# Pooled attention and two feed-forward layers on one core: float64 words of the first block combined in a PSUM bank

## The chip, the cores and the metric

The kernel runs on one core of a Trainium2 chip. Its time is the device time of one execution, in microseconds (us); the median of several runs is given. TensorE multiplies matrices and writes to PSUM, a memory of eight banks of 128 x 512 float32 values. VectorE (DVE in the profile), ScalarE (ACT) and GpSimd (POOL) work on tiles in SBUF; VectorE and ScalarE also read and write PSUM. Each engine takes its instructions in order. The queue of the DMAs of this kernel is nearly always that of SyncE (SP).

## The reference, cut to what matters

q, k and v are 8 x 8 x 576 x 64 (batch, heads, sequence, head size).

```python
k_p = k.reshape(B, H, 72, 8, D).mean(axis=3)
v_p = v.reshape(B, H, 72, 8, D).mean(axis=3)
scores = matmul(q, k_p.T) / sqrt(D)
attn = exp(scores - max(scores)); attn = attn / (sum(attn) + 1e-9)
x = matmul(attn, v_p)                      # 4608 tokens x 512
g = s * relu(x @ w_in) ** 2 + b            # 2048 wide
x = g @ w_out                              # 512 wide
out = (sigmoid(x @ w_gate) * (x @ w_val)) @ w_out2      # 1536 wide, then 512
```

The activations come in float32, the five weights as float64. The result is float32.

## The kernel before, in words

**Products.** Every float32 product is made of three: each operand is split into a high part, rounded to the format that TensorE multiplies at full rate, and a low part, which is what rounding left over; high x low, high x high and low x high are added up in PSUM. The helper `split` (lines 53 to 56) makes the two parts: ScalarE copies the value into `hi` (line 55), and VectorE or GpSimd, as the caller says, subtracts (line 56).

**Weights.** A float64 weight tile arrives as 128 x 1024 words of 32 bits (`load64`, three buffers `raw`). `convert` (lines 73 to 84) makes a float32 of each pair of words, `low` and `high`, which lie alternately in SBUF: ScalarE turns the high word's exponent and leading mantissa bits into the middle value `w` (line 80), VectorE shifts the low word in place (line 81), combines `w` and `low` (line 82), and combines `high`'s sign bit and `w` (line 83). `w` is a tile `cv` of SBUF (six buffers). Lines 82 and 83 read two tensors each, both in SBUF. The weights `w_in` and `w_out` of the first feed-forward layer, 16 tiles each, are converted while block 0 runs, and split with GpSimd's subtraction: `split_wi` (lines 129 to 135) and `split_wo` (148 to 153). The split `w_in` is stored to DRAM for the other blocks, `w_out` stays in SBUF. The second layer's weights are converted and stored in the same way later on (`prep_w2`, from step 18 on).

**Order of the work.** The 4608 tokens are nine blocks of 512. The first layer runs in 144 steps (block j, slice m of the 2048). A step is `emit_h` (lines 186 to 206: 12 products into `hps`, then on ScalarE the Relu that reads `hps`, line 200, and the rest of the activation), `split_g`, and, two steps later, `emit_x` (lines 218 to 237: 12 products into the four accumulators `acc`). Attention makes the tokens of the following block in units of 256 tokens, two per block, a few pieces in each step, as the table `events` says (lines 445 to 482): `scores` twice per 128 tokens (a product into `sps`, a maximum and a subtraction on VectorE that read it, lines 370 and 371), `norm` (the sum and its inverse on VectorE, the product on GpSimd), `left`, `turn` twice (transposes into `tm` and `tl`, read by a split and a copy), and `values` twice (a product into `pv`, read by a split into `xh` and `xl`). `pool_v_pe` adds up the pooled rows of v for batches 0 and 1 with TensorE, into `vps`; `place_v` and `place_left` read it. Units 0 and 1, for block 0 itself, and the first conversions come ahead, in a stage in which all engines keep the order of the program (line 492). Units 2 and 3 belong to the 16 steps of block 0, and step 16 needs both. After that stage and up to step 16 every engine's order is planned at build time from a model of the durations; from step 16 on TensorE's order is that of the program (line 604).

**PSUM.** The eight banks are three pools: `ps_a` has four (the accumulators, and the scores of the first stage), `ps_b` two (`hps`, and batch 0's `vps`), and `ps_c` two (`sps`, `tm`, `tl`, `pv`, batch 1's `vps`). In the second layer (`first_half`, `plain`) the last two pools give two banks each to the products there. Whoever takes a bank waits until the last reader of what it held is done.

Of the kernel before, what the change touches and what calls it, by code (L numbers as in the profile page):

```python
# [8 lines left out]
F32 = mybir.dt.float32  # L9
F32R = mybir.dt.float32r  # L10
I32 = mybir.dt.int32
# [8 lines left out]
def pooled_attention_two_ffn(ctx, tc, q, k, v, v_left, w_in, w_out, s_in, b_in, w_gate, w_val, w_out2, out):  # L20
# [22 lines left out]
    cvp = ctx.enter_context(tc.tile_pool(name="cvp", bufs=6))  # L43
    dram = ctx.enter_context(tc.tile_pool(name="dram", bufs=1, space=DRAM))
    ps_a = ctx.enter_context(tc.tile_pool(name="ps_a", bufs=4, space=PSUM))
    ps_b = ctx.enter_context(tc.tile_pool(name="ps_b", bufs=2, space=PSUM))
    ps_c = ctx.enter_context(tc.tile_pool(name="ps_c", bufs=2, space=PSUM))

    ident = const.tile([128, 128], F32, name="ident")
    s_sb = const.tile([128, 1], F32, name="s_sb")  # L50
    b_sb = const.tile([128, 1], F32, name="b_sb")

    def split(hi, lo, src, eng):

# [18 lines left out]
    def convert(raw, w):  # L73

        words = raw.rearrange("p (f two) -> p f two", two=2)
        low, high = words[:, :, 0], words[:, :, 1]
        nc.scalar.activation(out=w.bitcast(F32), in_=high.bitcast(F32), func=ACTF.Copy, scale=2.0**-112)  # L80
        nc.vector.tensor_scalar(out=low, in0=low, scalar1=29, scalar2=None, op0=ALU.logical_shift_right)
        nc.vector.scalar_tensor_tensor(out=w, in0=w, scalar=3, in1=low, op0=ALU.logical_shift_left, op1=ALU.bitwise_or)
        nc.vector.scalar_tensor_tensor(out=w, in0=high, scalar=-(2**31), in1=w, op0=ALU.bitwise_and, op1=ALU.bitwise_or)
        return w.bitcast(F32)

    def block_of(t):
# [52 lines left out]
    def store_later():  # L139
        while later:  # L140
            dst, t = later.pop(0)
            nc.sync.dma_start(out=dst, in_=t if t.dtype == F32 else t.bitcast(F32))
# [43 lines left out]
    def emit_h(i):  # L186
        j, m = steps[i]
        n = blocks[j][1]
        hi, lo = wi.pop(i)
        ps = ps_b.tile([128, 512], F32, tag="b", name="hps")[:, :n]  # L190
        a, c = x_tiles(j)
        step = UNIT if i < 2 else n
        for t0 in range(0, n, step):
            f = slice(t0, t0 + step)
            for kk in range(KD):
                nc.tensor.matmul(out=ps[:, f], lhsT=hi[:, kk], rhs=c[:, kk, f], start=kk == 0, stop=False)  # L196
                nc.tensor.matmul(out=ps[:, f], lhsT=hi[:, kk], rhs=a[:, kk, f], start=False, stop=False)  # L197
                nc.tensor.matmul(out=ps[:, f], lhsT=lo[:, kk], rhs=a[:, kk, f], start=False, stop=kk == KD - 1)  # L198
        g = gp.tile([128, 512], F32, tag="g", name="g", bufs=2)[:, :n]
        nc.scalar.activation(out=g, in_=ps, func=ACTF.Relu)  # L200
        if j == 0:
            nc.scalar.activation(out=g, in_=g, func=ACTF.Square)
        else:
            nc.vector.tensor_tensor(out=g, in0=g, in1=g, op=ALU.mult)  # L204
        nc.scalar.activation(out=g, in_=g, func=ACTF.Identity, scale=s_sb, bias=b_sb)  # L205
        g_t[i] = g
# [95 lines left out]
    def pool_v_pe(b, what):  # L302

        n = NP if what == "v" else 2
        ps = (ps_c if b else ps_b).tile([128, n, D], F32, tag="c" if b else "b", name="vps")
        f = ps.rearrange("p i d -> p (i d)")
        ts = [raws.pop((b, nm)) for nm in (("v0", "v1") if what == "v" else ("l",))]
        per = POOL // len(ts)
        for r in range(POOL):
            t = ts[r // per]  # L310
            nc.tensor.matmul(out=f, lhsT=ident, rhs=t[:, r % per * n * D:(r % per + 1) * n * D], start=r == 0, stop=r == POOL - 1)
        sums[b, what] = ps
# [43 lines left out]
    def scores(u, t, c, pool=None):  # L356
        if c == 0:
            s_t[u, t] = (at2.tile([128, H, SP], F32, tag="e", name="e"), at2.tile([128, H], F32, tag="mx", name="mx"))
        e, mx = s_t[u, t]
        ps = (ps_a if pool else ps_c).tile([128, 4, SP], F32, tag="a" if pool else "c", name="sps")  # L360
        for i in range(2):
            for off, n, b, _ in segs(u * UNIT + t * 128, 128):
                nc.tensor.matmul(
                    out=ps[off:off + n, 2 * i:2 * i + 2, :].rearrange("p h j -> p (h j)"),
                    lhsT=q_t[u][:, 2 * i + c, t * 128 + off:t * 128 + off + n],
                    rhs=kbd[b % 2][:, 2 * i + c].rearrange("p two j -> p (two j)"),
                    start=True, stop=True,
                )
        h = slice(4 * c, 4 * c + 4)
        nc.vector.tensor_reduce(out=mx[:, h], in_=ps, axis=AX.X, op=ALU.max)  # L370
        nc.vector.tensor_tensor(out=e[:, h], in0=ps, in1=mx[:, h].unsqueeze(2).to_broadcast([128, 4, SP]),
                                op=ALU.subtract)
        if c == 1:
            nc.scalar.activation(out=e, in_=e, func=ACTF.Exp, scale=1.0 / (POOL * float(D) ** 0.5))
            if t == 1:
                q_t.pop(u)
# [25 lines left out]
    def turn(u, t, part):  # L402
        if (t, part) == (0, 0):
            t_t[u] = (
                at1.tile([128, NP, UNIT], F32R, tag="t1", name="t1"),
                at1.tile([128, NP, UNIT], F32R, tag="t2", name="t2"),
                at1.tile([128, 2, UNIT], F32R, tag="t3", name="t3"),
            )
        t1, t2, t3 = t_t[u]
        c = slice(t * 128, t * 128 + 128)  # L410
        if part == 0:
            pm = e_t[u, t][0]
            tm = ps_c.tile([128, NP, 128], F32, tag="c", name="tm")
            for i in range(NP):
                nc.tensor.transpose(tm[:, 2 * (i % 2) + i // 2, :], pm[:, 2 * i:2 * i + 2, :].rearrange("p h j -> p (h j)"), ident)
            split(t1[:, :, c], t2[:, :, c], tm, nc.vector)
        else:
            lt = e_t.pop((u, t))[1]
            tl = ps_c.tile([128, 2, 128], F32, tag="c", name="tl")
            for cc in range(2):  # L420
                nc.tensor.transpose(tl[:, cc, :], lt[:, 4 * cc:4 * cc + 4].bitcast(F32).rearrange("p h s j -> p (h s j)"), ident)
            nc.scalar.activation(out=t3[:, :, c], in_=tl, func=ACTF.Copy)

    def values(u, cc):
        t1, t2, t3 = t_t[u]
        ps = ps_c.tile([128, 2, UNIT], F32, tag="c", name="pv")
        for i2 in range(2):
            i = 2 * cc + i2
            for off, n, b, _ in segs(u * UNIT, UNIT):
                f = slice(off, off + n)  # L430
                vh, vl, vr = v1h[b % 2], v1l[b % 2], v3[b % 2]
                o = ps[:, i2, f]
                nc.tensor.matmul(out=o, lhsT=vh[:, i], rhs=t2[:, i, f], start=True, stop=False)
                nc.tensor.matmul(out=o, lhsT=vl[:, i], rhs=t1[:, i, f], start=False, stop=False)
                nc.tensor.matmul(out=o, lhsT=vh[:, i], rhs=t1[:, i, f], start=False, stop=False)
                nc.tensor.matmul(out=o, lhsT=vr[:, cc, i2], rhs=t3[:, i2, f], start=False, stop=True)
        j, o = block_of(u * UNIT)
        a, c = x_tiles(j)
        f = slice(o, o + UNIT)
        split(a[:, 2 * cc:2 * cc + 2, f], c[:, 2 * cc:2 * cc + 2, f], ps, nc.vector)  # L440
        if cc == 1:
            t_t.pop(u)
# [47 lines left out]
        turn(u, t, 1)  # L490

    with tc.manual_schedule():
        load_kv(0, "k")
        load_q(0, 2)
        load_kv(0, "v")
# [44 lines left out]
    if True:  # L540
        values(1, 0)
        values(1, 1)
        split_wo(0)
        load_wi(2)
        load_q(2)
# [56 lines left out]
        for i in range(NS):  # L602
            if i == M1:
                pe_order.enter_context(tc.manual_schedule(engines={mybir.EngineType.PE}))
            store_later()
            for fn, args in events.pop(2 * i, []):
                fn(*args)
            load_wi(i + 3)
# [74 lines left out]

        def first_half(p, m):
            n = pairs[p][1]
            b0, b1 = (ps_b.tile([128, 512], F32, tag="b", name="pb")[:, :n] for _ in range(2))
            b2, b3 = (ps_c.tile([128, 512], F32, tag="c", name="pc")[:, :n] for _ in range(2))
            product(b0, p, m, A11, True, 0)
            p1 = wk.tile([128, 512], F32, tag="wk", name="wk")[:, :n]
            nc.scalar.activation(out=p1, in_=b0, func=ACTF.Copy)  # L690
# [38 lines left out]

        def plain(p, m):  # L730

            gate = ps_b.tile([128, 512], F32, tag="b", name="pb")
            val = ps_c.tile([128, 512], F32, tag="c", name="pc")
            product(gate, p, m, 2, True, 0)
            product(gate, p, m, 3, False, 1)
            product(val, p, m, 0, True, 0)
            product(val, p, m, 1, False, 1)
            gated(p, m, 0, gate, val)
# [77 lines left out]
```

## Time and profile before

| | |
|---|---|
| median of 3 runs | 1793.14 us (1792.07 to 1793.2) |
| span of the profiled execution | 1792.0 us (no other time of this execution is given) |
| TensorE busy | 1739.8 us, 97% |
| VectorE busy | 937.2 us, 52% |
| ScalarE busy | 774.8 us, 43% |
| GpSimd busy | 550.1 us, 31% |
| DMA, mean | 166 GB/s |

The span runs from the first to the last instruction of one execution; the runs that were timed are others. The shares are means over the whole execution, while the conversions of the first layer's weights all lie in its first 165 us. A row of the view by line gives a group of equal instructions with its count, the time in which any of them ran, the mean duration of one, and the idle time of the engine ahead of them. A row in order of time begins with the start and the duration in us; a bracket at its end gives the idle time before it and what ended that. Rows of one engine overlap by about 0.1 us, since the next instruction starts while the one before is still writing its last elements.

### The profile page before, as it was taken

The numbers are of one execution on the slowest core, as the hardware profiler recorded it, in microseconds if no ns is written. First come the engines' busy times: TensorE is split into PE (matmuls) and PEld (weight loads), VectorE is DVE, ScalarE is ACT, GpSimd is POOL, SyncE is SP. The second block draws the span as 40 slices with busy tenths as digits, with TensorE's granted clock in tenths as the row PEclk, the third lists the DMA queues.
The fourth block names the chain that finished last, engine by engine and source line by source line (L and its number), as shares of the span: only waits on it lengthen the run. The fifth ranks groups of instructions, "written<-read, shape, count | busy, mean of one in ns | idle before, by whom it ended". The sixth has DMA issues, their size and how long they took to land.

```text
span 1792.0 us, 21860 instructions
## 1 busy us (share of the span) xinstructions
PE 1739.8 (97%) x8064; PEld 1446.9 (81%) x8064; DVE 937.2 (52%) x1491; ACT 774.8 (43%) x1390; POOL 550.1 (31%) x592
## 2 busy tenths in 40 slices
PE   5788999999999999999999999999999999999999
PEld 4667888888888888888887888888888888888887
DVE  6897747556465656444443545554545454545111
ACT  2566444444444545444444434343424343444122
POOL 3764504224042322010002443144314431443132
PEclk8989999999999999999999999999999999999999
DMA  6776735647383736332433334733473347333642
GB/s 229 261 227 211 273 123 198 223 165 250 112 267 123 265 118 223 118 118 94 141 106 144 118 109 146 251 114 113 144 253 110 117 141 256 106 118 115 235 140 83
DMA packets 84282, 298.18 MB, mean 166 GB/s; under 512 B 9808, under 2 KB 10832, under 8 KB 84176
## 3 DMA queue, kind: packets, MB, share of 16 engines
q1 hardware_dynamic: 80976, 286.30, 46.7%
q0 software_dynamic: 3200, 10.49, 1.7%
q8 instruction: 64, 1.05, 0.2%
q14 instruction: 42, 0.34, 0.1%
HBM read 250.61 MB, written 46.14 MB: 166 GB/s over the span
## 4 chain that ended last, share of the span: by engine, by line
PE 72%; issue 4%; DMA 1%; POOL 1%; DVE 0%; ACT 0%; POOLq 0%; DVEq 0%
PE pc L664 5%; PE pc L663 5%; PE pc L662 5%; PE acc L718 5%; PE acc L720 5%; PE acc L719 5%; PE pb L664 4%; PE pb L663 4%; PE pb L662 4%; PE hps L196 4%; PE hps L198 4%; PE hps L197 4%; PE acc L227 4%; PE acc L229 4%; PE acc L228 4%
## 5 line engine op out<-in xcount | busy, mean ns | idle before, releaser
L56 POOL TENSOR_TENSOR w<-w 128x512 fp32r<-128x512 f32 x264 | 254.4, 996 | 505.2 <-ACT w L55 481.7
L668 DVE TENSOR_TENSOR wk<-pc,wk 128x512 f32<-128x512 f32 x192 | 132.3, 689 | 240.8 <-PE pc L664 240.7
L196 PE MATMUL hps<-xl,wi 128*128 128x512 f32 (+1 forms) x584 | 234.5, 402 | 5.5 <-ACT g L200 2.6
L198 PE MATMUL hps<-xh,wi 128*128 128x512 f32 (+1 forms) x584 | 227.4, 389 | 0.0
L197 PE MATMUL hps<-xh,wi 128*128 128x512 f32 (+1 forms) x584 | 227.1, 389 | 0.0
L227 PE MATMUL acc<-gl,woh 128*128 128x512 f32 x576 | 225.5, 391 | 0.2 <-DVE gl L56 0.2
L228 PE MATMUL acc<-gh,woh 128*128 128x512 f32 x576 | 225.2, 391 | 0.0
L229 PE MATMUL acc<-gh,wol 128*128 128x512 f32 x576 | 225.0, 391 | 0.0
L56 DVE TENSOR_TENSOR gl<-g,gh 128x512 fp32r<-128x512 f32 x204 | 156.7, 768 | 129.6 <-ACT gh L55 124.6
L55 ACT ACTIVATE gh<-g 128x512 fp32r<-128x512 f32 x204 | 128.2, 628 | 142.5 <-DVE g L680 139.7
L204 DVE TENSOR_TENSOR g<-g 128x512 f32<-128x512 f32 x128 | 97.9, 765 | 150.3 <-ACT g L200 150.3
L205 ACT ACTIVATE g<-g,b_sb,s_sb 128x512 f32<-128x512 f32 x144 | 117.3, 814 | 126.4 <-DVE g L204 125.6
L662 PE MATMUL pc<-xo,w 128*128 128x512 f32 x432 | 168.1, 389 | 0.0
L664 PE MATMUL pc<-xo,w 128*128 128x512 f32 x432 | 168.1, 389 | 0.0
L663 PE MATMUL pc<-xo,w 128*128 128x512 f32 x432 | 168.0, 389 | 0.0
L200 ACT ACTIVATE g<-hps 128x512 f32<-128x512 f32 x144 | 85.3, 593 | 176.5 <-PE hps L198 174.6
L55 ACT ACTIVATE w<-w 128x512 fp32r<-128x512 f32 x264 | 113.3, 503 | 100.4 <-DMA w<-w7d 100.4
L664 PE MATMUL pb<-xo,w 128*128 128x512 f32 x336 | 131.6, 392 | 1.7 <-POOL w L56 1.7
L196 PEld LDWEIGHTS hps<-xl,wi 128*128 128x128 f32 x584 | 111.0, 190 | 26.8 <-ACT g L200 2.8
L662 PE MATMUL pb<-xo,w 128*128 128x512 f32 x336 | 131.3, 391 | 0.5 <-ACT w L55 0.5
L663 PE MATMUL pb<-xo,w 128*128 128x512 f32 x336 | 131.2, 390 | 0.0
L198 PEld LDWEIGHTS hps<-xh,wi 128*128 128x128 f32 x584 | 110.6, 189 | 23.5
(113 smaller groups left out, 3245.5 us busy)
## 6 DMA issues: line engine op xcount, KB each, us to landing
wi<-w1d SPq DMA_DIRECT2D x128, 512.0 KB, 3.4
wo<-wo2d SPq DMA_DIRECT2D x108, 512.0 KB, 3.5
w<-w7d SPq DMA_DIRECT2D x48, 896.0 KB, 4.4
raw<-in SPq DMA_DIRECT2D x68, 512.0 KB, 4.6
kv<-in SPq DMA_DIRECT2D x24, 512.0 KB, 5.2
kv<-in SPq DMA_DIRECT2D x16, 576.0 KB, 4.7
cv<-x2d POOLq DMA_DIRECT2D x36, 256.0 KB, 5.9
out<-eo SPq DMA_DIRECT2D x36, 256.0 KB, 4.2
```

Of the source, the lines that this page charges most:

```text
L55: nc.scalar.activation(out=hi, in_=src, func=ACTF.Copy)
L56: eng.tensor_tensor(out=lo, in0=src, in1=hi.bitcast(F32), op=ALU.subtract)
L196: nc.tensor.matmul(out=ps[:, f], lhsT=hi[:, kk], rhs=c[:, kk, f], start=kk == 0, stop=False)
L197: nc.tensor.matmul(out=ps[:, f], lhsT=hi[:, kk], rhs=a[:, kk, f], start=False, stop=False)
L198: nc.tensor.matmul(out=ps[:, f], lhsT=lo[:, kk], rhs=a[:, kk, f], start=False, stop=kk == KD - 1)
L227: nc.tensor.matmul(out=acc[j][d], lhsT=hi[:, f], rhs=gl, start=m == 0, stop=False)
L228: nc.tensor.matmul(out=acc[j][d], lhsT=hi[:, f], rhs=gh, start=False, stop=False)
L229: nc.tensor.matmul(out=acc[j][d], lhsT=lo[:, f], rhs=gh, start=False, stop=m == M1 - 1)
L662: nc.tensor.matmul(out=ps, lhsT=w[:, 0, x, kk], rhs=r[:, 1, kk, :n], start=first and kk == 0, stop=False, skip_group_check=True)
L663: nc.tensor.matmul(out=ps, lhsT=w[:, 0, x, kk], rhs=r[:, 0, kk, :n], start=False, stop=False, skip_group_check=True)
L664: nc.tensor.matmul(out=ps, lhsT=w[:, 1, x, kk], rhs=r[:, 0, kk, :n], start=False, stop=kk == 1, skip_group_check=True)
L668: nc.vector.tensor_tensor(out=o, in0=ps, in1=b_, op=ALU.add)
```

## The change

The pools `ps_b` and `ps_c` become one pool of four banks with names of their own, `p0` to `p3`. A table `banks` says which of them serve the first product (`h`), attention (`at`) and conversions (`cv`) at a given point of the program; those of one kind are taken in turn. In the first stage `h` has bank 0, `cv` bank 1, and `at` banks 2 and 3. Behind the values of unit 1, `cv` has banks 1 and 2, and `at` bank 3. From step 16 on `h` has 0 and 1 and `at` has 2 and 3, as before, and `cv` none; conversions then use an SBUF tile again. Where `cv` has banks, the middle value of `convert` lies in one of them: line 80 writes it there, the first combination reads and writes it there, and the second reads it there and writes the result to the SBUF tile as before. The number of instructions and of DMAs stays the same.

```diff
-    ps_b = ctx.enter_context(tc.tile_pool(name="ps_b", bufs=2, space=PSUM))
-    ps_c = ctx.enter_context(tc.tile_pool(name="ps_c", bufs=2, space=PSUM))
+    ps_b = ctx.enter_context(tc.tile_pool(name="ps_b", bufs=1, space=PSUM))
...
+    banks = {"h": (0, 1), "at": (2, 3), "cv": ()}
+    turns_of = {}
+
+    def bank(kind, shape, name, dtype=F32):
+
+        x = turns_of[kind] = turns_of.get(kind, -1) + 1
+        return ps_b.tile(shape, dtype, tag=f"p{banks[kind][x % len(banks[kind])]}", name=name)
...
-        nc.scalar.activation(out=w.bitcast(F32), in_=high.bitcast(F32), func=ACTF.Copy, scale=2.0**-112)
+        e = bank("cv", [128, 512], "cvps", I32) if banks["cv"] else w
+        nc.scalar.activation(out=e.bitcast(F32), in_=high.bitcast(F32), func=ACTF.Copy, scale=2.0**-112)
         nc.vector.tensor_scalar(out=low, in0=low, scalar1=29, scalar2=None, op0=ALU.logical_shift_right)
-        nc.vector.scalar_tensor_tensor(out=w, in0=w, scalar=3, in1=low, op0=ALU.logical_shift_left, op1=ALU.bitwise_or)
-        nc.vector.scalar_tensor_tensor(out=w, in0=high, scalar=-(2**31), in1=w, op0=ALU.bitwise_and, op1=ALU.bitwise_or)
+        nc.vector.scalar_tensor_tensor(out=e, in0=e, scalar=3, in1=low, op0=ALU.logical_shift_left, op1=ALU.bitwise_or)
+        nc.vector.scalar_tensor_tensor(out=w, in0=high, scalar=-(2**31), in1=e, op0=ALU.bitwise_and, op1=ALU.bitwise_or)
...
-        ps = ps_b.tile([128, 512], F32, tag="b", name="hps")[:, :n]
+        ps = bank("h", [128, 512], "hps")[:, :n]
...
-        ps = (ps_c if b else ps_b).tile([128, n, D], F32, tag="c" if b else "b", name="vps")
+        ps = bank("at" if b else "h", [128, n, D], "vps")
...
-        ps = (ps_a if pool else ps_c).tile([128, 4, SP], F32, tag="a" if pool else "c", name="sps")
+        ps = ps_a.tile([128, 4, SP], F32, tag="a", name="sps") if pool else bank("at", [128, 4, SP], "sps")
...
-            tm = ps_c.tile([128, NP, 128], F32, tag="c", name="tm")
+            tm = bank("at", [128, NP, 128], "tm")
...
-            tl = ps_c.tile([128, 2, 128], F32, tag="c", name="tl")
+            tl = bank("at", [128, 2, 128], "tl")
...
-        ps = ps_c.tile([128, 2, UNIT], F32, tag="c", name="pv")
+        ps = bank("at", [128, 2, UNIT], "pv")
...
     with tc.manual_schedule():
+        banks.update(h=(0,), cv=(1,))
         load_kv(0, "k")
...
         values(1, 0)
         values(1, 1)
+        banks.update(cv=(1, 2), at=(3,))
         split_wo(0)
...
             store_later()
+            if i == M1:
+                banks.update(h=(0, 1), at=(2, 3), cv=())
             for fn, args in events.pop(2 * i, []):
...
```

In `first_half` and `plain` the tiles of the second layer's products come from `bank("h", ...)` and `bank("at", ...)`, two banks each, in place of the two pools.

## Rows read from the trace of the kernel before

**Rows 1.** Busy time by stage: PE, PEld, DVE, ACT, POOL, clock, DMA, GB/s.

```profile
0.00:60.00 60.00, 36.51 (x192) 32.23 (x192) 41.85 (x86) 19.91 (x39) 23.64 (x36) 0.80 0.69 238
60.00:165.00 105.00, 85.26 (x402) 68.78 (x403) 99.87 (x139) 70.08 (x129) 72.01 (x58) 0.95 0.73 244
165.00:240.00 75.00, 75.00 (x373) 63.38 (x372) 46.97 (x78) 36.60 (x64) 28.65 (x32) 1.00 0.63 220
240.00:1792.00 1552.00, 1543.03 (x7100) 1282.49 (x7098) 748.50 (x1189) 648.19 (x1160) 425.80 (x467) 1.00 0.46 156
```

**Rows 2.** VectorE by line, 60 to 165 us: count, busy us, mean ns, idle.

```profile
L83 DVE SCALAR_TENSOR_TENSOR cv<-raw,cv 128x512 int32<-128x512 int32 x24 | 24.7, 1028 | 0.3
L82 DVE SCALAR_TENSOR_TENSOR cv<-cv,raw 128x512 int32<-128x512 int32 x24 | 24.4, 1015 | 2.4 <-ACT cv L80 2.0
```

**Rows 3.** Line 56, 60 to 165 us: count, minimum/median/maximum ns, first, last start.

```profile
L56 POOL TENSOR_TENSOR wol<-cv,woh x14: 1270/1596/1746, 58.9 to 161.6; 128x512 fp32r<-128x512 f32 x14
...
L56 DVE TENSOR_TENSOR gl<-g,gh x13: 677/683/1779, 70.1 to 161.9; 128x512 fp32r<-128x512 f32 x13
L56 DVE TENSOR_TENSOR t<-tm,t x4: 632/657/692, 94.7 to 163.6; 128x512 fp32r<-128x512 f32 x4
```

**Rows 4.** Tile `cv` from 60 to 165 us, same columns.

```profile
L80 ACT ACTIVATE cv<-raw x24: 648/668/696, 61.2 to 156.6; 128x512 f32<-128x512 f32 x24
L82 DVE SCALAR_TENSOR_TENSOR cv<-cv,raw x24: 676/766/1790, 61.9 to 159.1; 128x512 int32<-128x512 int32 x24
```

**Rows 5.** In order of time near 95 us: start us, duration us.

```profile
95.25 1.29 POOL L56 TENSOR_TENSOR wi<-cv,wi 128x512 fp32r<-128x512 f32 x1
...
95.66 1.44 DVE L82 SCALAR_TENSOR_TENSOR cv<-cv,raw 128x512 int32<-128x512 int32 x1 [0.30 <-ACT cv L80]
```

**Rows 6.** In order of time, TensorE and then VectorE, 17 to 27 us.

```profile
17.77 1.95 PE L311 MATMUL vps<-kv,ident 128*128 128x128 f32 x16
19.55 1.15 PE L363 MATMUL sps<-kbd,qT 128*128 128x144 f32 x8
...
24.46 0.43 DVE L56 TENSOR_TENSOR v1l<-vps,v1h 64x256 fp32r<-64x256 f32 x1 [0.45 <-ACT v1h L55]
...
25.90 0.46 DVE L370 TENSOR_REDUCE mx<-sps 128x4 f32<-128x288 f32 x1
```

**Rows 7.** In order of time, TensorE, then ScalarE: steps 2 and 13.

```profile
62.40 0.50 PE L196 MATMUL hps<-xl,wi 128*128 128x512 f32 x1 [2.58 <-ACT g L200]
...
65.02 0.39 PE L198 MATMUL hps<-xh,wi 128*128 128x512 f32 x1
...
159.01 0.39 PE L198 MATMUL hps<-xh,wi 128*128 128x512 f32 x1
...
161.95 0.39 PE L196 MATMUL hps<-xl,wi 128*128 128x512 f32 x1
...
71.43 0.59 ACT L200 ACTIVATE g<-hps 128x512 f32<-128x512 f32 x1
...
162.32 0.60 ACT L200 ACTIVATE g<-hps 128x512 f32<-128x512 f32 x1
```

**Rows 8.** Waits from 60 to 165 us: us in total, times, longest us.

```profile
ACT woh L55 <- DVE cv L83: 16.6, 6, 6.6
...
ACT wi L55 <- DVE cv L83: 7.2, 6, 2.1
```

**Rows 9.** In order of time: attention of unit 3, then scores of block 1.

```profile
123.07 1.30 PE L363 MATMUL sps<-kbd,qT 128*128 128x144 f32 x4 [2.81 <-issue]
...
130.88 0.44 DVE L371 TENSOR_TENSOR e<-sps,mx 128x288 f32<-128x288 f32 x1
...
169.00 0.69 DVE L56 TENSOR_TENSOR xl<-pv,xh 128x512 fp32r<-128x512 f32 x1 [2.07 <-ACT xh L55]
...
275.83 1.15 PE L363 MATMUL sps<-kbd,qT 128*128 128x144 f32 x8
...
277.51 0.81 DVE L371 TENSOR_TENSOR e<-sps,mx 128x288 f32<-128x288 f32 x2
```

More of the change, by code (lines that the diff above doesn't have):

```diff
@@ L685, in first_half @@
             n = pairs[p][1]
-            b0, b1 = (ps_b.tile([128, 512], F32, tag="b", name="pb")[:, :n] for _ in range(2))
-            b2, b3 = (ps_c.tile([128, 512], F32, tag="c", name="pc")[:, :n] for _ in range(2))
+            b0, b1 = (bank("h", [128, 512], "pb")[:, :n] for _ in range(2))
+            b2, b3 = (bank("at", [128, 512], "pc")[:, :n] for _ in range(2))
             product(b0, p, m, A11, True, 0)
@@ L730, in plain @@
         def plain(p, m):
-            gate = ps_b.tile([128, 512], F32, tag="b", name="pb")
-            val = ps_c.tile([128, 512], F32, tag="c", name="pc")
+            gate = bank("h", [128, 512], "pb")
+            val = bank("at", [128, 512], "pc")
             product(gate, p, m, 2, True, 0)
```

## The prediction, made before the changed kernel was run

> **What bounds the kernel now.** I read the windows by stage first [rows 1]. From 165 us to 240 us TensorE is busy 75.00 of 75.00 us, and 1543.03 of 1552 after that, so whatever happens before 165 us shifts the rest as a block and the change is worth what it moves the moment at which TensorE becomes continuously busy. From 60 to 165 us TensorE is busy 85.26 of 105 us at a mean granted clock of 0.95 (of the two levels 2.4 and 1.2 GHz, the lower one for part of the time), VectorE 99.87, ScalarE 70.08, GpSimd 72.01. VectorE limits this stretch; the 19.7 us of TensorE's idle time and some 4.3 us lost to the clock (5% of 85.26) are the most that can come back there, 24.0 us. Before 60 us VectorE is busy 41.85 of 60: waits of single instructions set the pace, not its sum.
>
> What fills VectorE is the next view, its instructions by line in that stretch [rows 2]: lines 82 and 83, the two that combine the words of a float64 weight, have a mean of 1015 and 1028 ns, 24 times each. The spread of one line says why [rows 3, 4]. Line 82 goes from 676 ns to 1790. `gl`, also two SBUF inputs, goes from 677 to 1779. `t<-tm,t`, one input in PSUM and one in SBUF, keeps between 632 and 692 in the same stretch. One collision in order of time [rows 5]: GpSimd's split of `wi` runs from 95.25 to 96.54 us, line 82 starts at 95.66 and takes 1.44 us, which is 0.88 us of waiting and 0.68 of work after GpSimd is done (the rows overlap by about 0.1). GpSimd is held up in turn (`wol` 1270 ns at best, 1596 in the median). So a VectorE instruction with two SBUF inputs and a GpSimd one shut each other out, and one with a single SBUF input isn't touched.
>
> **The change, part by part.**
>
> *The conversion's middle word lies in PSUM.* Nothing is added or dropped; lines 82 and 83 each keep one SBUF input (`low`, `high`) and take the other from PSUM. If they then behave like `t<-tm,t`, each falls to some 0.69 us: 24 x (1.015 + 1.028 - 1.380) = **15.9 us** less VectorE time between 60 and 165 us, which fits into the 24.0 that TensorE can give back. The eight conversions before 60 us I count as nothing, since VectorE is not the limit there. The collisions of `gl` and of other two-input instructions stay.
>
> *The price of PSUM itself.* No row shows VectorE writing to PSUM, which line 82 will do. From below: `t<-tm,t` against the best `gl`, 657 - 677 ns, would be 48 x -0.02 = -1.0 us. From above: the part of an instruction that does not grow with its elements, paid once more by line 82. The split `v1l` of 256 elements takes 0.43 us [rows 6] against `gl`'s 677 ns for 512, which is 0.96 ns an element and leaves 0.18 us that is fixed: 24 x 0.18 = +4.4 us. I take 0, the nearest row being `t<-tm,t`. The Trainium skill's page VectorE: DVE Perf Modes (section on the TRN2 errata) gives 120 fixed cycles to an instruction from PSUM against 58 from SBUF; at its 0.96 GHz that estimate is 65 ns each, 3.1 us for the 48, and the sum by it would be 3.1 us worse. The medians above, 657 and 683 ns, speak against it.
>
> ScalarE's line 80 now writes to PSUM: 668 ns today [rows 4], and its nearest row is a Relu out of PSUM, 0.59 to 0.60 [rows 7]; 24 x 0.08 = 1.9 us either way. I take 0, because ScalarE has 35 us of slack there; without that slack it would be these 1.9 us.
>
> *Two banks for the conversions instead of six SBUF tiles.* Line 80 of one conversion must now wait for line 83 of the one before last, and behind it in ScalarE's queue stand the Relu and the splits that release TensorE and GpSimd. Two conversions through one bank are 0.67 + 0.69 + 0.69 = 2.1 us of hold each; they come every 105/24 = 4.4 us. I take 0, with 0 to 2 for the range.
>
> *One bank for the first product.* This is the term I trust least. Line 196 of a step can't start until the Relu (line 200) of the step before has read the bank. In [rows 7] the product of step 2 starts at 62.40 and ends at 65.41, its Relu starts at 71.43, a lag of 6.0 us; of step 13 the product ends at 159.40 and the Relu starts at 162.32, a lag of 2.9. Over the 12 steps 2 to 13 the lags sum to 60.1 us, 5.0 each. With one bank a step can't be shorter than 3.0 (product) + lag + 0.6 (Relu) + 0.1 (hand-over: step 2 started 0.06 us after the Relu that it waited for had ended) = 3.7 + lag. The 12 steps from 62.40 to 161.95 take 8.30 us each now, so the bank starts to hurt at a lag of 4.6. The Relu is late because ScalarE works in order and waits for line 83: 16.6 + 7.2 = 23.8 us in 12 waits [rows 8]. If each microsecond that VectorE saves comes off these waits, the lag becomes 5.0 - 15.9/12 = 3.7 and the step 7.4 us. VectorE alone would allow (99.55 - 15.9)/12 = 7.0. So the bank gives back 12 x 0.43 = **+5.1 us**. Bounds: 0, if all of these waits go (lag 3.0), and the whole 15.9 and 5 more, if the lag stays.
>
> *The start.* The pooling of batch 0 (`v`, then the rest `l`) shares bank 0 with the product. In [rows 6] TensorE begins `l` at 17.77; now it must wait until `v` has been split, at 24.89 (24.46 + 0.43). Then 1.95 us for `l`, and half of the 1.15 us of the scores queued behind it: their first maximum starts at 27.4 instead of 25.90, **+1.5 us**, and everything up to about 50 us is a fixed order behind it. The first half of step 1's product, which runs today while unit 1's values are not there yet, moves behind the Relu of step 0: 12 products of half width, half of the 3.0 us of a whole one [rows 7], **+1.5**. Together +3.0, between 0 (the idle time of 60 - 36.51 us in that stage takes it in) and +4.
>
> *One bank for attention after that.* Twenty tiles of units 2 and 3 (scores, transposes, values), and batch 1's pooling, go through one bank. In [rows 9] the first score tile of unit 3 is written at 123.07 and given free at 131.32, 8.3 us; the unit ends at 169.69 after ten tiles in 46.6 us. When VectorE is not backed up, two score tiles take 275.83 to 278.32, 1.25 us each. Average holds above 4.7 us would delay the unit, and step 16 with it. I take +1, from 0 to +9 (two thirds of 8.3 us, ten times, less 46.6).
>
> **Sum**: -15.9 + 0 + 0 + 5.1 + 3.0 + 1.0 = -6.8 us. The span of the profiled execution is 1792.0 and the runs lie between 1792.07 and 1793.2, so about 1 us lies around the span; against the median of 1793.14 the forecast is **1786 us**.
>
> **The rivals.**
>
> *The products' bank sets the pace (slower).* Place: line 196 waiting for line 200, steps 2 to 13. If ScalarE's order keeps the Relu behind the weights' splits, the lag stays 5.0, the step becomes 8.7, 12 x 0.4 = +5, and with the start's 3.0 it is 1801. It decides from a lag of 4.6. For it: the lag is 6.0 already at step 2. Against it: outside the fixed part the order is planned at build time with this new wait in it, so the Relu may stand further ahead in ScalarE's queue, and at step 13 the lag is 2.9.
>
> *The freed time is eaten (no change).* `gl`, the in-place shift of line 81 and the small splits still collide with GpSimd, which has 72 us of its own to run; if they get half of the blocking that lines 82 and 83 lose, 8.0 us are left, the lag is 4.3, the step 8.0 and the gain 3.6, just eaten by the start and attention: 1793. It also covers that a PSUM operand does not free these lines. Against it: `t<-tm,t`.
>
> *The Relu comes forward too (faster still).* The lag falls below 3.2, VectorE's full 15.9 counts, the start costs 3 and attention nothing: 1780.
>
> **How the numbers follow.** Forecast 0.40, slower rival 0.22, no change 0.18, faster still 0.20. 0.2%, 3.6 us, is about what a measurement of this kernel can tell from no change. Faster: the 0.20 and 0.36 of the forecast's 0.40, 0.56. Same: the 0.04 that is left of it and 0.14 of the no-change case, 0.18. Slower: the first rival's 0.22 and the other 0.04 of the no-change case, where attention's bank adds its 9 us, 0.26. The range runs from the faster case with 5 us of unknown costs in its favour, 1775, to the slower case, 1801. The likeliest case alone is 1781 to 1791.
>
> **What would show it.** Right: lines 82 and 83 between 0.65 and 0.75 us with a small spread; VectorE below 90% busy in the stretch; TensorE continuously busy some 7 us sooner; step 1's product entirely behind the first Relu. Wrong: those lines still up to 1.7 us; TensorE waiting for line 200 with many microseconds in the list of waits; the maxima and subtractions of the scores as releasers of TensorE; step 16's product waiting for the last `xl`.

## The result, and the profile after

The changed kernel takes 1807.26 us (median of 4 runs, 1805.48 to 1809.48), the kernel before 1792.61 beside it on the same chip. The ratio is 1.0085, with a 95% interval from 1.0073 to 1.0097: about 15 us **slower**, where 1786 us, 7 us faster, was forecast. The profiled execution took 1807.5 us, its span is 1805.7. In the listing of the changed kernel the lines lie 7 to 8 further down: the conversion's 80 to 83 are now 88 to 91, the splits' 55 and 56 are 62 and 63, the product's 196 and Relu's 200 are 204 and 208, scores are 371 (read by 378 and 379), the values' four products 441 to 444.

Busy time by stage, the changed kernel (columns as in [rows 1]):

```profile
0.00:60.00 60.00, 35.93 (x159) 32.81 (x160) 36.51 (x80) 18.50 (x37) 21.52 (x35) 0.74 0.58 211
60.00:165.00 105.00, 93.00 (x438) 75.23 (x437) 86.40 (x137) 71.17 (x128) 61.21 (x56) 0.95 0.74 262
165.00:190.00 25.00, 14.81 (x65) 11.76 (x64) 8.86 (x18) 7.80 (x15) 14.02 (x18) 0.74 0.41 143
190.00:240.00 50.00, 50.00 (x239) 41.91 (x238) 31.17 (x56) 24.08 (x42) 13.52 (x15) 0.96 0.64 222
240.00:1806.00 1566.00, 1556.13 (x7170) 1293.25 (x7169) 752.42 (x1202) 655.50 (x1169) 426.97 (x469) 1.00 0.45 155
```

From 60 to 165 us it goes as forecast: VectorE falls from 99.87 to 86.40 us (82%), TensorE rises from 85.26 to 93.00. Then comes a hole that before does not have: from 165 to 190 us TensorE is busy 14.81 of 25 us, at a granted clock of 0.74, where before it was busy without a break [rows 1]. The loss lies there.

The conversion's lines, in the tile `cvps` and on VectorE, 60 to 165 us (columns as in [rows 4]):

```profile
L88 ACT ACTIVATE cvps<-raw x26: 610/634/679, 60.2 to 148.6; 128x512 f32<-128x512 f32 x26
L90 DVE SCALAR_TENSOR_TENSOR cvps<-cvps,raw x26: 681/694/700, 60.9 to 150.3; 128x512 int32<-128x512 int32 x26
L91 DVE SCALAR_TENSOR_TENSOR cv<-raw,cvps x26: 631/682/690, 61.6 to 151.5; 128x512 int32<-128x512 int32 x26
```

No collision is left in them: 700 ns at most, where line 82 went up to 1790 [rows 4]. The overlaps with GpSimd bear this out. In the trace of before, 23 of the 48 instructions of lines 82 and 83 took 0.83 us or more, and each of these overlapped GpSimd's work for longer than its excess over 0.68 us. In the changed kernel 26 of the 52 still overlap it by more than 0.3 us, and none is longer for it. Line 63 shows who still collides and who gained (same stretch and columns):

```profile
L63 DVE TENSOR_TENSOR gl<-g,gh x14: 679/686/1780, 63.8 to 159.6; 128x512 fp32r<-128x512 f32 x14
...
L63 POOL TENSOR_TENSOR wol<-cv,woh x14: 1277/1362/1737, 64.2 to 153.6; 128x512 fp32r<-128x512 f32 x14
```

`gl`, with both inputs in SBUF, is held up as before; GpSimd's `wol` has come from a median of 1596 ns to 1362 [rows 3].

The hole, in order of time (start us, duration us; in brackets the idle time ahead and what ended it):

```profile
138.56 0.27 PE L444 MATMUL pv<-t,v 128*128 128x192 f32 x1
144.58 0.58 ACT L62 ACTIVATE xh<-pv 128x512 fp32r<-128x512 f32 x1
148.44 0.68 DVE L63 TENSOR_TENSOR xl<-pv,xh 128x512 fp32r<-128x512 f32 x1
150.14 0.65 PE L371 MATMUL sps<-kbd,qT 128*128 128x144 f32 x4
...
172.26 0.63 PE L423 MATMUL tm<-ident,pm 128*128 128x128 f32 x4 [1.13 <-DVE e L379]
174.79 0.44 PE L429 MATMUL tl<-ident,lt 128*128 128x128 f32 x2 [1.90 <-DVE t L63]
179.76 0.69 PE L429 MATMUL tl<-ident,lt 128*128 128x128 f32 x2 [1.41 <-DVE t L63]
180.92 0.58 PE L441 MATMUL pv<-t,v1h 128*128 128x256 f32 x1 [0.47 <-ACT t L430]
183.27 0.31 ACT L337 ACTIVATE lh<-s 128x128 fp32r<-128x128 f32 x1 [2.40 <-POOL s L277]
184.84 0.58 PE L441 MATMUL pv<-t,v1h 128*128 128x256 f32 x1 [1.85 <-DVE xl L63]
187.59 0.69 DVE L63 TENSOR_TENSOR xl<-pv,xh 128x512 fp32r<-128x512 f32 x1 [2.79 <-ACT xh L62]
188.33 1.33 PE L371 MATMUL sps<-kbd,qT 128*128 128x144 f32 x4 [1.41 <-DVE xl L63]
189.28 0.80 PE L204 MATMUL hps<-xl,wi 128*128 128x512 f32 x1
```

The first four lines are the cause, the rest what it does. The first row is the last of the 16 products of unit 2's last value tile, which began at 136.91. The tile is written by 138.84, and its bank is given free only when `xl` has been split, at 149.12; then, at 150.14, unit 3's first score tile goes into the same bank. Before, that tile stood there at 123.07 [rows 9]. From 171 us on TensorE works at nothing but unit 3's chain, one tile after the other: transpose, split, transpose, copy, values, split. (Within it 2.4 us pass while ScalarE, in order, stands at line 337 waiting for GpSimd.) TensorE could have had other work: the 24 products into `acc` of steps 14 and 15, whose `gl` is there from 167.42 and 175.63 on. But from step 16 on TensorE's order is that of the program, and there they stand behind step 16's product (the first of them starts at 194.25). How much of the hole they would have filled, no run shows. Step 16's product, which needs the last `xl`, starts at 189.28; step 15's had started at 167.75. These 21.5 us between two steps were 6.3 in the trace of before (170.72 and 177.05).

### The profile page after: what moved, and what is told of

It reads as the page before. It is cut to its first block, busy times and chain, and to the rows that moved or that the text cites. A ratio compares the mean times of both kernels' runs of the same rounds, so it can differ in the third digit from the quotient of the medians.

```text
span 1805.7 us, 21850 instructions
## 1 busy us (share of the span) xinstructions
PE 1749.9 (97%) x8064; PEld 1455.0 (81%) x8064; DVE 915.4 (51%) x1491; ACT 777.0 (43%) x1390; POOL 537.2 (30%) x592
## 4 chain that ended last, share of the span: by engine, by line
PE 84%; issue 5%; DMA 4%; DVE 4%; POOL 1%; ACT 1%; DVEq 0%; POOLq 0%; SPq 0%; ACTq 0%
PE hps L204 6%; PE hps L206 6%; PE hps L205 6%; PE acc L235 6%; PE acc L236 6%; PE acc L237 6%; PE pc L674 5%; PE pc L676 5%; PE pc L675 5%; PE acc L730 5%; PE acc L732 5%; PE acc L731 5%; PE pb L676 4%; PE pb L674 4%; PE pb L675 4%
## 5 line engine op out<-in xcount | busy, mean ns | idle before, releaser
L63 DVE TENSOR_TENSOR gl<-g,gh 128x512 fp32r<-128x512 f32 x204 | 151.5, 743 | 122.1 <-ACT gh L62 117.2
L235 PEld LDWEIGHTS acc<-gl,woh 128*128 128x128 f32 x576 | 108.7, 189 | 29.7 <-DVE gl L63 7.6
```

The source lines that it names most:

```text
L63: eng.tensor_tensor(out=lo, in0=src, in1=hi.bitcast(F32), op=ALU.subtract)
L235: nc.tensor.matmul(out=acc[j][d], lhsT=hi[:, f], rhs=gl, start=m == 0, stop=False)
```

## The experiments

The changed kernel is three things at once: conversions through PSUM, one bank for the products (`h` in the table of banks), one bank for attention (`at`). The theory after the result: attention's bank opens the hole, by some 15 us, and the other two about cancel. The rival: the bank of the products, with the start, costs most, and the hole is only where the delay is seen. All edits are in the table of banks (e11 also passes each unit's number along); the first `update` stands at the head of the first stage, the second behind the values of unit 1. Edits are against the changed kernel, those of e12 and e13 against e10. Differences between two kernels are taken from their ratios to before, times 1793 us.

**e1: attention gets its second bank back.**

```diff
-        banks.update(cv=(1, 2), at=(3,))
+        banks.update(cv=(1,), at=(2, 3))
```

> The changed kernel with attention given back its two banks in block 0; conversions then have one bank, the product still one. Theory A (attention's one bank makes the units follow each other, and unit 3 ends late): the hole of TensorE ahead of step 16 goes, step 16 starts no later than before (177 us), 1785 to 1793 us. Theory B (the product's one bank costs the time): stays above 1800. Theory C (conversions lack banks): slower than the changed kernel, above 1808.

Measured: 1790.69 us, ratio to before 0.9979 [0.9970, 0.9989], some 19 us less than the changed kernel. Windows of this kernel:

```profile
60.00:165.00 105.00, 94.52 (x479) 77.54 (x477) 88.97 (x151) 76.25 (x139) 64.64 (x62) 0.98 0.74 255
165.00:190.00 25.00, 22.65 (x95) 18.47 (x96) 16.18 (x23) 11.77 (x20) 13.89 (x16) 0.93 0.74 270
```

The hole has all but closed (22.65 of 25 us), and step 16 starts at 174.66, 3.6 us after step 15. The conversions have one bank here instead of two and hardly miss the other: from 60 to 165 us line 88 waits for a line 91 twice, 2.4 us in all, against once, 1.3 us, in the changed kernel.

**e2: attention's one bank alone**, conversions in SBUF and two banks for the products, as before.

```diff
-        banks.update(h=(0,), cv=(1,))
...
-        banks.update(cv=(1, 2), at=(3,))
+        banks.update(at=(3,))
```

> The kernel before with one bank for attention in block 0 behind the first stage, and nothing else: two banks for the product, conversions through SBUF (the bank left over is unused). Theory A: the hole ahead of step 16 is there without any conversion in PSUM, 1803 to 1815 us, and longer than in the changed kernel because VectorE still collides. Theories B and C: no change, 1790 to 1796.

Measured: 1811.89 us, 1.0091 [1.0073, 1.0110]: +16.3 us from this edit alone. The hole is longer than in the changed kernel, from step 15 at 162.30 to step 16 at 194.32:

```profile
165.00:190.00 25.00, 12.42 (x54) 9.15 (x52) 12.27 (x25) 7.31 (x14) 13.25 (x17) 0.68 0.42 131
```

**e3: the products' one bank alone**, from the first stage on.

```diff
-        banks.update(h=(0,), cv=(1,))
+        banks.update(h=(0,))
...
-        banks.update(cv=(1, 2), at=(3,))
```

> The kernel before with one bank for the product up to step 16, from the first stage on, and nothing else. Theory A: 1793 to 1800 us, the first stage's share (batch 0's pooled v in the same bank) and no more, since the changed kernel's Relu followed its product at once in most steps. Theory B: above 1803.

Measured: 1805.80 us, 1.0066 [1.0046, 1.0085], +11.8 us: what Theory B gave, and more than was expected. There is no hole (step 15 at 182.02, step 16 at 185.72); step 2 already starts at 70.53 instead of 62.40. From e3 to e1 only the conversions move to PSUM, and the ratio falls by 0.0087, 15.6 us.

**e4: two banks for the products from the second stage on**, attention still with one.

```diff
-        banks.update(cv=(1, 2), at=(3,))
+        banks.update(h=(0, 1), cv=(2,), at=(3,))
```

> The changed kernel with two banks for the product in block 0, one for conversions and one for attention. Theory A: the hole stays, 1800 to 1810 us. Theory B: gone, below 1795. Theory C: above 1810.

Measured: 1797.57 us, 1.0012 [0.9999, 1.0024]. That is 13 us better than the changed kernel and outside all three ranges, again more than expected for this bank (the conversions have one bank less here). Step 2 starts at 57.95, ten microseconds earlier than in the changed kernel, and the hole is there (step 15 at 159.25, step 16 at 174.75), shorter than with one bank for the products.

Both theories had something: attention's bank makes the hole, and the products' bank costs nearly as much, early. The next two take the start apart.

**e5: first stage as before, then e1's banks. e9: first stage as before, then the change's.**

```diff
-        banks.update(h=(0,), cv=(1,))
...
-        banks.update(cv=(1, 2), at=(3,))
+        banks.update(h=(0,), cv=(1,), at=(2, 3))
```

> The kernel e1 (one bank for the product, one for conversions, two for attention) with the first stage as before the change, so that the pooled v of batch 0 has two banks and the first two conversions go through SBUF. If the first stage carries at least half of the 11 us of the product's one bank: 1783 to 1787 us. If the step by step wait of the product for the Relu carries it: 1789 to 1792, as e1.

```diff
-        banks.update(h=(0,), cv=(1,))
...
-        banks.update(cv=(1, 2), at=(3,))
+        banks.update(h=(0,), cv=(1, 2), at=(3,))
```

> The changed kernel with the first stage as before the change; attention keeps one bank and the product one from then on. First stage's share: if it is 4 us or more, 1799 to 1803 us; if nothing, 1805 to 1809. Attention's hole ahead of step 16 stays in either case.

Measured: e5 1788.07 us, 0.9961 [0.9948, 0.9974], between what the two theories gave; e9 1801.48, 1.0042 [1.0025, 1.0058], within its range. Against the changed kernel e9 saves 0.0043, 7.7 us, by the first stage alone. e5 against e1 saves some 3 us, but their intervals overlap.

**e6 and e8: no group loses a bank; the conversions share one**, in e6 with the products (`h` 0 and 1, `cv` 1), in e8 with attention (`at` 2 and 3, `cv` 3). The first stage is as before.

```diff
-        banks.update(h=(0,), cv=(1,))
...
-        banks.update(cv=(1, 2), at=(3,))
+        banks.update(cv=(1,))
```

> First stage as before the change; then in block 0 two banks for the product, two for attention, and conversions in bank 1, which they share with the product in turn. Theory so far, from the four runs before: conversions in PSUM are worth some -15 us (two pairs that differ in that alone: e1 against e3, e4 against e2), attention's one bank costs some +17, the product's one bank some +11. With no bank taken away for good, 1778 to 1787 us. Rival (a shared bank is as bad as one bank, since every second product must wait for a conversion and the conversion for the Relu): 1789 us or more.

```diff
-        banks.update(h=(0,), cv=(1,))
...
-        banks.update(cv=(1, 2), at=(3,))
+        banks.update(cv=(3,))
```

> As the run above, but conversions share bank 3 with attention. If holds of attention (some 8 us each) are what makes its banks scarce, conversions wait behind them and hold up ScalarE: 1788 to 1800 us, slower than the run above. If the program's order of attention's tiles in one bank is what costs, a bank that is shared only now and then costs little: 1778 to 1787.

Measured: e6 1818.68 us, 1.0132 [1.0116, 1.0149]; e8 1821.59, 1.0150 [1.0132, 1.0168]: the slowest of all, and neither near the hoped-for time. The pair e4 and e2 in e6's expectation differs in the first stage too, so that figure rests on e1 and e3. From the list of waits from 50 to 220 us, e8 (us in total, times, longest):

```profile
PEld hps L204 <- ACT wi L62: 20.5, 6, 7.4
PE hps L204 <- ACT wi L62: 18.9, 6, 7.1
```

In e8 the products wait for weights that are split too late. The list of e6 has another head: VectorE waits 32.2 us for the words of the weights to arrive. A bank that two jobs use in turn ties their orders together: a conversion stands between two tiles of the other job and can't be taken ahead of them. That this is the chain behind the 24 and 27 us was not isolated by a run.

**e10: two banks for the products through steps 0 and 1, the conversions into PSUM from step 2, attention with two banks throughout.**

```diff
-        banks.update(h=(0,), cv=(1,))
...
-        banks.update(cv=(1, 2), at=(3,))
...
+            if i == 2:
+                banks.update(h=(0,), cv=(1,))
```

> The best kernel so far (e5: first stage as before, then one bank for the product, one for conversions, two for attention), with the one bank for the product and the conversions in PSUM from step 2 on only; steps 0 and 1 as before the change. If the product's one bank costs its time in steps 0 and 1, where step 1 waits for step 0's Relu: step 2 starts at 58 to 62 us instead of 65.25, and 1780 to 1785 us. If it costs in the steps after: no better than e5, 1786 to 1790.

Measured: **1783.93 us, 0.9938 [0.9925, 0.9951]**: 11 us below before and 26 below the changed kernel, the best of the study. Step 2 starts at 60.15, as the first theory had it. Windows, and the product of step 16 in order of time:

```profile
60.00:165.00 105.00, 95.69 (x467) 78.34 (x465) 88.85 (x151) 74.70 (x137) 65.28 (x65) 0.98 0.73 258
165.00:190.00 25.00, 24.10 (x113) 20.11 (x114) 19.17 (x27) 13.48 (x24) 17.38 (x19) 1.00 0.86 291
```

```profile
165.90 0.50 PE L204 MATMUL hps<-xl,wi 128*128 128x512 f32 x1 [1.30 <-ACT g L208]
```

No hole, the full clock, step 16 at 165.90 (changed kernel 189.28, before 177.05).

**e12: as e10, and the products' second bank back at step 15 instead of 16.**

```diff
-            if i == M1:
+            if i == M1 - 1:
```

> As e10, with the second bank of the product given back at step 15 instead of 16, since no conversion of the first layer's weights is left by then. Up to 2 us better than e10 (in e5 step 16 waited for step 15's Relu, 2.4 us behind the end of its product), or the same.

Measured: 1784.38 us, 0.9946 [0.9933, 0.9959], the same as e10.

**e13: as e10, with the conversions left in SBUF.** This prices the collisions by themselves.

```diff
             if i == 2:
-                banks.update(h=(0,), cv=(1,))
+                banks.update(h=(0,))
```

> The best kernel e10 (two banks for attention throughout, one for the product from step 2 on) with its conversions left in SBUF, as before the change; bank 1 then stands empty up to step 16. It differs from e10 in the place of the middle word alone. Theory (the collisions of the two combinations with GpSimd cost what the sum had, 15.9 us): 1796 to 1802 us, lines 90 and 91 up to 1.7 us each again. Rival (the other way of handing out banks, and not the collisions, is what made e10 fast): 1782 to 1787.

Measured: 1798.07 us, 1.0026 [1.0015, 1.0038]. Against e10 the ratio is 0.0088 higher, 15.8 us. VectorE's two lines, 60 to 165 us (columns as in [rows 2]), first e13, then e10:

```profile
L90 DVE SCALAR_TENSOR_TENSOR cv<-cv,raw 128x512 int32<-128x512 int32 x24 | 25.8, 1080 | 3.2 <-ACT cv L88 3.0
L91 DVE SCALAR_TENSOR_TENSOR cv<-raw,cv 128x512 int32<-128x512 int32 x24 | 19.7, 825 | 0.3
```

```profile
L90 DVE SCALAR_TENSOR_TENSOR cvps<-cvps,raw 128x512 int32<-128x512 int32 x25 | 17.3, 694 | 6.6 <-ACT cvps L88 6.4
L91 DVE SCALAR_TENSOR_TENSOR cv<-raw,cvps 128x512 int32<-128x512 int32 x25 | 17.0, 680 | 0.3
```

Between the starts of step 2 and step 15 lie 114.0 us in e13 and 101.6 in e10. Of the 15.8 us, the two lines' own time is 24 x (1.080 + 0.825 - 0.694 - 0.680) = 12.7 us. Against before, e13 is also the price of the products' one bank from step 2 on, with the conversions in SBUF: 0.26%, 4.7 us.

**e11: one bank for each unit of attention**, the second one taken from the conversions; the rest as in the changed kernel. This asks whether the hole comes from a unit having but one bank, or from unit 3 standing behind unit 2 in it. (The lines lie 2 further down.)

```diff
+        if kind == "at" and banks.get("own"):
+            return ps_b.tile(shape, dtype, tag=f"p{banks['own'][unit % 2]}", name=name)
...
-        banks.update(cv=(1, 2), at=(3,))
+        banks.update(cv=(1,), own=(3, 2))
```

> The changed kernel with a bank of its own for each unit of attention in block 0: unit 2 and batch 1's pooled v keep bank 3, unit 3 gets bank 2, conversions keep bank 1 alone. Each unit still has one bank. Theory O (the order between the units: unit 3's first scores stand behind unit 2's last values in the one bank): unit 3's first scores start before unit 2's values, the hole ahead of step 16 falls below 5 us, 1788 to 1796 us. Rival T (the turnaround of each tile inside a unit): the hole stays above 10 us, 1800 or more.

Measured: 1793.89 us, 1.0002 [0.9992, 1.0012], 15 us better than the changed kernel. Unit 3's first scores and step 16's first product, in order of time:

```profile
53.19 1.16 PE L373 MATMUL sps<-kbd,qT 128*128 128x144 f32 x4
...
173.14 0.80 PE L206 MATMUL hps<-xl,wi 128*128 128x512 f32 x1
```

Unit 3 now starts at 53.19 us, ahead of unit 2 (67.45), and step 16 follows step 15 after 9.3 us. With one bank each, both units end in time for step 16 to start sooner than before (177.05); so it is the queue of both through one bank that opens the hole. e1's alternating pair is still 4 us better.

## Why the prediction was wrong

The three terms, each measured alone: conversions in PSUM -15.8 us (e13 to e10; -15.6 from e3 to e1), attention's bank +16.3 (e2), the products' bank with the start +11.8 (e3). They add up to +12.3, each measured in other surroundings; the change itself gave about +15. The forecast was -15.9, +1.0 and +8.1.

- **Collisions, -15.9: right**, in mechanism and size. The lines run at 694 and 680 ns, and the time between steps 2 and 15 shrinks by 12.5 us (e13 and e10). That the size fits to 0.1 us is luck: between e13 and e10 the two lines themselves give back 12.7 us, and the rest comes from elsewhere (the shift, line 89, falls from 824 to 651 ns in the mean).
- **Price of PSUM, 0: right.** Line 90 writes and reads PSUM in 681 to 700 ns; without a collision line 82 took 676 at best [rows 4]. The estimate of 65 ns an instruction that I worked out from the Trainium skill, VectorE: DVE Perf Modes (TRN2 errata), does not show: 694 against 676 leaves 18. ScalarE's line 88 is faster into PSUM, 634 ns against 668.
- **Two conversion banks, 0: right**, within its 0 to 2: line 88 waited for a bank once, 1.3 us. Even one bank does (e1, e10).
- **One bank for attention, +1.0 with a ceiling of 9: the step that failed.** I asked whether the ten tiles of unit 3 fit into the 46.6 us that they had [rows 9]. I took the start of unit 3 as given and put at nothing its wait for what stands ahead of it in the one bank, in the order of the program: unit 2's ten tiles and the pooled `l` of batch 1. The first score tile of unit 2, before and then in the changed kernel:

```profile
57.60 0.71 PE L363 MATMUL sps<-kbd,qT 128*64 128x144 f32 x8
```

```profile
67.54 0.71 PE L371 MATMUL sps<-kbd,qT 128*64 128x144 f32 x8
```

From there to unit 3's first score tile at 150.14 these eleven tiles take 82.6 us; with two banks they took 65.5 (57.60 to 123.07). Unit 3 itself kept well below my limit of 4.7 us a tile (38.1 us for ten, 150.14 to 188.28), but by then it was 27 us late. The holds are not what I had wrong: I let them shrink to two thirds as VectorE emptied, and from first write to last read the eleven were held for 9.5 us on average before and 4.7 now (the longest, the last `pv`, for 12 us, from 136.91 to 149.12). That is 51 us in all. For the other 31 of the 82.6 us the bank stood empty until the next tile in the program's order came, and unit 3 could not slip in. What made each of these gaps was not isolated. The sign I had named as "step 16's product waiting for the last `xl`" is the one that came.
- **One bank for the products, +5.1: near in size** from step 2 on (4.7, e13, with the conversions in SBUF; no run prices it with them in PSUM), **by luck**. My sum had a lag of 3.7 us from product to Relu set the pace. In the changed kernel the lags over steps 2 to 13 sum to 17.9 us, 1.5 each, and in e13 to 28.9, 2.4 each; by my own formula the bank would then cost nothing. Only two of the products of steps 3 to 15 start within 0.1 us of the Relu before, in either kernel. What does cost the 4.7 us stays open. The slower rival's mechanism did not act either, as it decided from a lag of 4.6; it had the right side, for another reason.
- **The start, +3.0 with a ceiling of 4: mis-sized.** The products' bank costs 11.8 - 4.7 = 7.1 us before step 2 (e3 and e13, give or take 4), and the changed kernel's step 2 starts 5.8 us later than before (68.18 and 62.40). The pooled `l` waited as forecast, but it then ran slowly. TensorE in a window of before, 17 to 20 us, and in one of the changed kernel, 20 to 30 us, then the changed kernel in order of time:

```profile
17.00:20.00 3.00, 3.00 (x29) 3.00 (x28) 0.28 (x1) 0.00 (x0) 0.00 (x0) 1.00 0.93 379
```

```profile
20.00:30.00 10.00, 5.90 (x27) 5.92 (x28) 5.23 (x12) 2.39 (x6) 7.59 (x12) 0.50 0.43 165
```

```profile
24.10 3.75 PE L319 MATMUL vps<-kv,ident 128*128 128x128 f32 x16 [6.55 <-issue]
27.64 2.13 PE L371 MATMUL sps<-kbd,qT 128*128 128x144 f32 x8
...
28.85 0.46 DVE L378 TENSOR_REDUCE mx<-sps 128x4 f32<-128x288 f32 x1 [3.87 <-PE sps L371]
```

The same 16 products took 1.95 us in [rows 6]. I had moved their start and kept their duration; there the granted clock was 1.00, and here, after 6.55 us of idle time, it is 0.50, the lower level, and the first maximum starts at 28.85 instead of my 27.4. The rest would lie in steps 0 and 1: step 1's first product starts at 60.21, behind the first Relu (57.51), as forecast, and step 2's at 68.18. Either half of the change can be taken back alone with much of that effect: step 2 starts at 57.95 in e4 (the change's first stage, two banks behind it) and at 63.37 in e9 (first stage as before, one bank behind it). What each is worth by itself is not settled.

## What to carry to other kernels

Here, moving one operand of a two-input VectorE instruction to PSUM left no collision with GpSimd in it and gave back 15.6 and 15.8 us, but the bank that it takes must come from a job whose tiles aren't on the way to a deadline. To price a bank taken away, follow every tile that passes through it from the first to the one with the deadline, not only the tiles of the job that is late, and count with the holds the time in which the bank stands empty because the next tile in the queue isn't ready. Where a bank must be given up, take it from a job after its fixed start (e10), and don't queue independent chains in one bank: a bank for each took back 15 us here (e11), two in turn 19 (e1).

## What the runs showed of the hardware

In this kernel a delay cost TensorE twice, because it came back at the lower of its two levels of the granted clock: 3.75 us instead of 1.95 for the pooled `l` after 6.55 idle microseconds, and 5.1 instead of 3.0 for step 16's product (189.28 to 194.42), which follows the hole:

```profile
180.00:190.00 10.00, 6.26 (x24) 5.17 (x24) 1.97 (x4) 1.78 (x4) 5.83 (x9) 0.50 0.19 59
```

That is the window ahead of step 16 in the changed kernel: 6.26 of 10 us busy, granted clock 0.50, which is 1.2 GHz.
